# First loads of an attention kernel in order of need, and modulation columns turned on VectorE

## The chip, the cores and the metric

The kernel runs on one core of one Trainium2 chip. The metric is the device time of one execution in microseconds (us). Times of a trace are counted from its first instruction; the span of a trace (first to last instruction) is about 1.3 us shorter than the time of the same run. Each time below is a median of several executions. "Half clock" below means that the trace shows a granted TensorE clock of 0.50 of full speed.

## The reference, cut to what matters

```python
mod = (_silu(c) @ w_mod).reshape(c.shape[0], 6, 1, -1)      # c: 1 x 640, w_mod: 640 x 3840
sa, ca, ga, sb, cb, gb = (mod[:, i] for i in range(6))       # cut: written out in the reference
h = _layernorm(x) * (1 + ca) + sa                            # x: 1 x 2048 x 640
x = x + ga * _A_ref(h, A_k_cache, A_v_cache, A_wq, A_wo)     # 32 heads of 128, 2048 keys each
h = _layernorm(x) * (1 + cb) + sb
return x + gb * _B_ref(h, B_w1, B_w2, B_w3, B_w4)            # a smaller gated part, not touched here
```

`_A_ref` is attention: queries `h @ wq`, scores against the keys of the head, softmax, a weighted sum of the head's values, and the output weights `wo`. It is nearly all of the time. Of the six modulation rows, `sa` and `ca` are needed at once; the other four are needed only late.

## The kernel before

Instructions are not written in order. A helper records each one, `P.op(engine, function, estimated ns, reads, writes, priority, ...)`, and a scheduler of the kernel's own puts them in order and adds the waits. `from_slot(n)` means "not before the n-th exponential on ScalarE", counted from 0; there are `NP` = 8 exponentials for each step of one head and 512 queries. The parts that the change and the argument touch:

```python
def load_k(h, prio, gate=(), need=()):      # the keys come transposed, in four transfers on SP's queue
    b = h % NKV                             # NKV = 5 buffers for keys and values
    for i in range(4):
        dmaT(lambda e, i=i: e.dma_start_transpose(K_ap[b][:, i * 512:(i + 1) * 512].unsqueeze(1), A_k_cache[0, h, i * 512:(i + 1) * 512, :]),
             128, gate if i or h else (), (K[b][i],), prio + (1.6 if h == 0 and i else 0) + 0.01 * i, need)

def load_v(h, prio, eng="SP", gate=(), need=(), after=()):   # the values come as they lie, 512 KB in one transfer
    b = h % NKV
    dma(eng, lambda e: e.dma_start(V_ap[b][:, :, 0:128], A_v_cache[0, h].rearrange("(t p) d -> p t d", p=128)), 512, gate, (V[b],), prio, need, after)

# inside load_head(h): wm[2] is a part of the first modulation weights
if h in (1, 2, 3):
    load_k(h, (-294, -291, -289)[h - 1], (wm[2],), () if h < 3 else from_slot(12))
    load_v(h, (-292, -290, -289.5)[h - 1], gate=(wm[2],))

# the input of the late modulation, 640 values of bfloat16, goes to DRAM and comes back on all 128 partitions
def s_rows(slot):
    dma("SP", lambda e: e.dma_start(s_scr.ap().rearrange("(k p) -> p k", p=128), s_bf.ap, allow_slow_non_contiguous=True), 80, (s_bf,), (s_line,), slot * 1.0, from_slot(slot))
    dma("SP", lambda e: e.dma_start(s_row.ap, s_scr.ap().unsqueeze(0).to_broadcast([128, D])), 160, (s_line,), (s_row,), slot * 1.0)

# the matmul that needs the values: every one of a head waits for the head's whole buffer V[b]
P.op("PE", pv, 2 * MM(129), (pt, V[b]), (o[bk],), kb, accum=True)
# ... cut: scores, exponentials, output projection, normalisation, the second part and the tail
```

## Time and profile before

| what | value |
|---|---|
| time | 1377.84 us (1377.21 to 1378.32), three runs |
| the run that the profile shows | 1380.32 us, span 1379.0, mean granted TensorE clock 0.996 |
| TensorE busy | 99% of the span |
| stop 1, 18.33 to 21.80 us | values of head 0, then half clock to 27.4 |
| stop 2, 113.69 to 116.28 us | all engines quiet, then half clock to 119.5 |

The lines are in the prediction. They are read from the engine that is nearly always busy (TensorE) to its few stops, and from each stop to what ended it and to the clock behind it.

### The profile page before, as it was taken

The page shows a single profiled execution, that of the slowest core. Times are in us where ns is not written, and L with a number is a line of the kernel's source. Part 1 is how long each engine was busy: PE and PEld are TensorE (multiplying, and loading weights), DVE is VectorE, ACT ScalarE, POOL GpSimd, SP SyncE. Part 2 cuts the span into 40 slices and gives each one's busy share as a digit, 9 for nine tenths or more (in the row PEclk, how much of TensorE's full clock was granted, in tenths as well). Part 3 has the DMA queues.
Part 4 walks back from the last instruction along what each step waited for, and adds up shares of the span by engine and source line. Part 5 has one row for each costly group of instructions (what it writes and reads, how often), then busy time and mean ns, then how long its engine had stood idle before and what let it go on. Part 6 is the DMA issues. An engine that isn't in the chain of part 4 may idle for free.

```text
span 1379.0 us, 29901 instructions
## 1 busy us (share of the span) xinstructions
PE 1368.1 (99%) x13099; PEld 944.8 (69%) x13099; DVE 567.5 (41%) x1431; ACT 1101.6 (80%) x1144; POOL 107.1 (8%) x93
## 2 busy tenths in 40 slices
PE   8999999999999999999999999999999999999999
PEld 6766777677767777767776677767667766655665
DVE  4452444453333233233323332332333245799563
ACT  4987888888888888888888888888888888833322
POOL 0000000000000000000000000000333237500000
PEclk9999999999999999999999999999999999999999
DMA  9662624354213322151215121422227100441110
GB/s 203 121 119 44 121 42 81 83 106 81 47 35 62 82 46 37 24 97 35 39 32 108 36 47 36 85 59 47 55 56 125 43 13 16 113 88 41 42 44 31
DMA packets 273596, 90.39 MB, mean 66 GB/s; under 512 B 253425, under 2 KB 271538, under 8 KB 273458
## 3 DMA queue, kind: packets, MB, share of 16 engines
q1 hardware_dynamic: 270034, 85.75, 31.4%
q10 hardware_dynamic: 3280, 2.00, 0.7%
q8 instruction: 104, 1.70, 0.5%
q0 software_dynamic: 144, 0.66, 0.2%
q14 instruction: 34, 0.28, 0.1%
HBM read 41.68 MB, written 2.63 MB: 32 GB/s over the span
## 4 chain that ended last, share of the span: by engine, by line
PE 98%; DMA 1%; DVE 1%; ACT 0%; issue 0%; POOL 0%; POOLq 0%
PE f_O L799 34%; PE f_S L780 32%; PE f_M L704 10%; PE f_M L734 10%; PE f_S L976 2%; PE f_M L976 2%; PE f_O L963 2%; PE f_S L963 2%; PE f_S L914 1%; DMA f_KV<-in_A_v_cache_dram 1%; PE f_S L937 1%; PE f_M L937 1%; PE f_O L914 1%; DVE f_small L497 0%; PE f_S L438 0%; PE f_O L734 0%
## 5 line engine op out<-in xcount | busy, mean ns | idle before, releaser
L782 ACT ACTIVATE f_PQ<-f_S 128x1024 bf16<-128x1024 f32 x1024 | 1041.6, 1024 | 148.6 <-PE f_S L780 135.3
L799 PEld LDWEIGHTS f_O<-f_KV,f_PQ 128*128 128x128 bf16 x8192 | 591.9, 98 | 235.2 <-DMA f_KV<-in_A_v_cache_dram 4.0
L780 PE MATMUL f_S<-f_PQ,f_KV 128*128 128x512 bf16 x2048 | 728.6, 380 | 3.0 <-ACT f_PQ L782 3.0
L799 PE MATMUL f_O<-f_KV,f_PQ 128*128 128x129 bf16 x8192 | 715.1, 220 | 3.5 <-DMA f_KV<-in_A_v_cache_dram 3.5
L742 DVE TENSOR_TENSOR f_y<-f_M,f_y 128x320 f32<-128x320 f32 x192 | 94.4, 492 | 507.2 <-PE f_M L734 507.2
L734 PE MATMUL f_M<-f_wo,f_OO 128*128 128x320 bf16 x992 | 272.9, 299 | 0.0
L780 PEld LDWEIGHTS f_S<-f_PQ,f_KV 128*128 128x128 bf16 x2048 | 197.1, 98 | 32.4 <-ACT f_PQ L782 4.1
L704 PE MATMUL f_M<-f_hT,f_wq 128*128 128x512 bf16 (+1 forms) x640 | 175.8, 378 | 0.2 <-DVE f_tmp L745 0.2
L734 PEld LDWEIGHTS f_M<-f_wo,f_OO 128*128 128x128 bf16 x992 | 96.2, 98 | 28.5
L808 DVE TENSOR_TENSOR f_OO<-f_O,f_rl 128x256 bf16<-128x256 f32 x256 | 108.4, 423 | 8.2
L708 DVE CAST f_PQ<-f_M 128x512 bf16<-128x512 f32 x127 | 87.8, 691 | 53.6 <-PE f_M L704 53.1
L536 POOL TENSOR_TENSOR f_y<-f_y,f_mod 128x640 f32<-128x640 f32 x32 | 49.1, 1542 | 782.3 <-DVE f_y L742 782.3
L704 PEld LDWEIGHTS f_M<-f_hT,f_wq 128*128 128x128 bf16 x640 | 62.4, 98 | 63.8 <-DVE f_tmp L745 0.6
L806 DVE RECIPROCAL f_rl<-f_O 128x2 f32<-128x2 f32 x256 | 43.5, 170 | 39.1 <-PE f_O L799 34.9
L966 ACT ACTIVATE f_OO<-f_S 128x512 bf16<-128x512 f32 x28 | 16.7, 597 | 43.6 <-PE f_S L963 43.6
L740 DVE COPY f_y<-f_M 128x320 f32<-128x320 f32 x32 | 15.7, 492 | 55.3 <-PE f_M L734 52.0
L497 DVE BATCH_NORM_STATS2 f_small<-f_y 128x6 f32<-128x320 f32 (+1 forms) x72 | 32.5, 480 | 9.4 <-DMA f_y<-in_A_x_dram 7.6
L976 PE MATMUL f_M<-f_KV,f_OO 128*128 128x320 bf16 x224 | 31.7, 299 | 0.0
L976 PE MATMUL f_S<-f_KV,f_OO 128*128 128x320 bf16 x224 | 31.7, 299 | 0.0
L542 ACT ACTIVATE f_xn<-f_y,f_small 128x640 bf16<-128x640 f32 x10 | 9.1, 915 | 25.7 <-DVE f_small L521 25.7
L648 DVE TENSOR_REDUCE f_small<-f_tmp 128x1 f32<-128x640 f32 x20 | 16.4, 820 | 29.9 <-ACT f_PQ L782 29.9
L966 ACT ACTIVATE f_OO<-f_O 128x512 bf16<-128x512 f32 x28 | 16.7, 596 | 14.1 <-PE f_O L963 14.1
(140 smaller groups left out, 529.6 us busy)
## 6 DMA issues: line engine op xcount, KB each, us to landing
f_KV<-in_A_v_cache_dram SPq DMA_DIRECT2D x31, 512.0 KB, 4.7
f_wo<-in_A_wo_dram SPq DMA_DIRECT2D x8, 640.0 KB, 4.2
f_wq<-in_A_wq_dram SPq DMA_DIRECT2D x7, 640.0 KB, 4.5
f_xin<-in_A_x_dram SPq DMA_DIRECT2D x13, 320.0 KB, 3.8
out_dram<-f_xin SPq DMA_DIRECT2D x15, 160.0 KB, 1.8
f_KV<-in_B_w_dram SPq DMA_DIRECT2D x5, 432.0 KB, 3.9
f_KV<-in_A_k_cache_dram SPq DMA_TRANSPOSE x128, 2.7
f_OO<-f_OO SPq DMA_TRANSPOSE x128, 2.5
```

Of the source, the lines that this page charges most:

```text
L536: P.op(eng, lambda e: e.tensor_tensor(out=out, in0=a, in1=b, op=op), COST[eng][0], rd, wr, prio, lat=300 if eng == "POOL" else None, dual= ...
L704: P.op("PE", lambda e, i=i, kk=kk, mm=mm, a=a, z=z: e.matmul(mm[:, 0:z - a], wq_t[g % 2][:, kk, hh * 128:(hh + 1) * 128], hT_t[ch][:, kk, ...
L708: P.op("DVE", lambda e: e.tensor_copy(q.ap, m.ap), 690, (m,), (q,), s * NP - 90)
L734: P.op("PE", lambda e, m=m, qt=qt, hf=hf, hh=hh: e.matmul(m[:, 0:HD], OT_ap[gs][:, qt, hh, :], wo_t[g % 2][:, hh, hf * HD:(hf + 1) * HD], ...
L742: P.op("DVE", lambda e, m=m, yt=yt: e.tensor_tensor(out=yt.ap, in0=m[:, 0:HD], in1=yt.ap, op=ALU.add), 490, (m, yt), (yt,), s * NP - 60)
L780: P.op("PE", lambda e, sp=sp, r=r, kt=kt: e.matmul(sp[:, r * QC:(r + 1) * QC], K_ap[b][:, kt * 128:(kt + 1) * 128], q.ap, start=True, stop ...
L782: x = P.op("ACT", lambda e, sp=sp, pt=pt: e.activation(pt.ap.rearrange("p k q -> p (k q)"), sp.ap, ACT.Exp, scale=SCALE), 1021, (sp,), (pt ...
L799: ins = e.matmul(o[bk][:, w * 129:w * 129 + 129], pt[:, r, qt * 128:(qt + 1) * 128], V_ap[b][:, u, 0:129], start=(u == 0 and w == 0), stop ...
L806: P.op("DVE", lambda e, ov=ov, i0=i0: e.reciprocal(rl_t[:, i0:i0 + 2].unsqueeze(2), ov[:, 0:258].rearrange("p (u d) -> p u d", u=2)[:, :, ...
L808: evac.append(P.op("DVE", lambda e, ov=ov, i0=i0, bk=bk: e.tensor_tensor(out=On_ap[gs][:, 2 * bk:2 * bk + 2, hh, :], in0=ov[:, 0:258].rear ...
L963: P.op("PE", lambda e, m=m, f=f, kk=kk: e.matmul(m.ap, w3_ap[:, kk, f * 128:(f + 1) * 128], nT_ap[ch][:, kk, :], start=(kk == 0), stop=(kk ...
L976: P.op("PE", lambda e, f=f, hf=hf: e.matmul(m[:, hf * 512:hf * 512 + HD], gT_ap[:, f, i * 128:(i + 1) * 128], w4_ap[f][:, hf * HD:(hf + 1) ...
```

## The change

The intent is to take away both stops.

- **First loads in order of need.** The values of head 0 come in two halves, and the early matmuls wait for the first half alone. The keys of heads 1 and 2 and their values wait for the first exponential. Query weights of heads 2 and 3, and the second chunk of the input, are held back too, and the first keys of head 0 now wait for a part of the modulation weights, as its other keys did. The values of head 3, which stood in SP's queue ahead of that chunk's transposes, now stand behind them and behind the keys of head 3.
- **Modulation.** The input is no longer sent through DRAM two bytes at a time. It is computed again, on all partitions, from a broadcast of `c`: an exponential on ScalarE, then three VectorE operations on 128x640. The finished columns are turned by one VectorE transpose and written in four pieces. The broadcast is released at exponential 64, where the two-byte write had been released at 70.

```diff
-    load_v(0, -296.5, "ACT", after=(ln0[1],))
+    for a, z, t in ((0, NKT // 2, v0a), (NKT // 2, NKT, V[0])):
+        dma("ACT", lambda e, a=a, z=z: e.dma_start(V_ap[0][:, a:z, 0:128], A_v_cache[0, 0, a * 128:z * 128].rearrange("(t p) d -> p t d", p=128)),
+            256, (), (t,), -296.5, after=(ln0[1],))
...
-            load_k(h, (-294, -291, -289)[h - 1], (wm[2],), () if h < 3 else from_slot(12))
-            load_v(h, (-292, -290, -289.5)[h - 1], gate=(wm[2],))
+            load_k(h, (-294, -291, -289)[h - 1], need=from_slot((0, 0, 12)[h - 1]))
+            load_v(h, (-292, -290, -288)[h - 1], need=from_slot((0, 0, 12)[h - 1]))
...
-    load_wq(0, 1, HG, -296.8, eng="ACT", after=(ln0[0],))
+    load_wq(0, 1, 2, -296.8, eng="ACT", after=(ln0[0],))
+    load_wq(0, 2, HG, -291, eng="POOL", need=from_slot(1))
...
-                640, (wm[3], wm[4]), xs + held, -294)
+                640, (), xs + held, -292, need=(lambda: ln0[2],))
...
-                    P.op("PE", pv, 2 * MM(129), (pt, V[b]), (o[bk],), kb, accum=True)
+                    P.op("PE", pv, 2 * MM(129), (pt, v0a if s == 0 and u < NKT // 2 else V[b]), (o[bk],), kb, accum=True)
...
     def s_rows(slot):
-        (the two-byte write and its read back, shown above)
+        c_bf = T(flat(nTx_t)[:, D:2 * D])
+        dma("SP", lambda e: e.dma_start(c_bf.ap, c[0:1, :].to_broadcast([128, D])), 160, (), (c_bf,), slot * 1.0, from_slot(slot))
+        P.op("ACT", lambda e: e.activation(tmp[0].ap, c_bf.ap, ACT.Exp, scale=-1.0), act(D), (c_bf,), (tmp[0],), slot + 9.0, need=from_slot(slot + 9))
+        P.op("DVE", lambda e: e.tensor_scalar_add(out=tmp[1].ap, in0=tmp[0].ap, scalar1=1.0), 600, (tmp[0],), (tmp[1],), slot + 12.0, need=from_slot(slot + 12))
+        P.op("DVE", lambda e: e.reciprocal(tmp[0].ap, tmp[1].ap), 825, (tmp[1],), (tmp[0],), slot + 14.0, need=from_slot(slot + 14))
+        P.op("DVE", lambda e: e.tensor_tensor(out=s_row.ap, in0=tmp[0].ap, in1=c_bf.ap, op=ALU.mult), 825, (tmp[0], c_bf), (s_row,), slot + 20.0, dual=True, need=from_slot(slot + 20))
... cut: the columns of all four rows in one tile `cols`, its transpose and the four writes; small bookkeeping
```

More of the change, by code (lines that the diff above doesn't have):

```diff
@@ L406, in fast_path @@
                                            fill=1.0, base=0, channel_multiplier=1), 300, (ident,), (ident,), -298)
+    v0a = T()
     def v_ones(i):
-        P.op("POOL", lambda e: e.memset(V_ap[i][:, :, 128:130], 1.0), 200, (), (V[i],), -297 + i)
+        P.op("POOL", lambda e: e.memset(V_ap[i][:, :, 128:130], 1.0), 200, (), (V[i],) + ((v0a,) if i == 0 else ()), -297 + i)
     for i in range(NKV):
@@ L587, in ln1 @@
                 if k % 2:
-                    P.op("ACT", lambda e, k=k: e.activation(hT_t[0][:, k, :], hslice(k, 0, 4), ACT.Identity,
+                    h = P.op("ACT", lambda e, k=k: e.activation(hT_t[0][:, k, :], hslice(k, 0, 4), ACT.Identity,
                                                             scale=caT[:, k:k + 1], bias=saT[:, k:k + 1]),
                          770, (hp[k], saT, caT), (hT[0][k],), -280 + k)
+                    ln0.append(h)
                 else:
@@ L607, in load_k @@
             dmaT(lambda e, i=i: e.dma_start_transpose(K_ap[b][:, i * 512:(i + 1) * 512].unsqueeze(1), A_k_cache[0, h, i * 512:(i + 1) * 512, :]),
-                 128, gate if i or h else (), (K[b][i],), prio + (1.6 if h == 0 and i else 0) + 0.01 * i, need)
+                 128, gate, (K[b][i],), prio + (1.6 if h == 0 and i else 0) + 0.01 * i, need)
     def load_v(h, prio, eng="SP", gate=(), need=(), after=()):
@@ L627, in fast_path @@
     ln1(0, -280)
-    s_scr = nc.dram_tensor("s_scratch", [D], BF16)
     m_scr = nc.dram_tensor("m_scratch", [4, D], F32)
-    s_line, s_row = T(), T(flat(nTx_t)[:, 0:D])
+    s_row = T(flat(nTx_t)[:, 0:D])
     nT_old[3] = lambda: (s_row,)
     wT = [[T() for _ in range(KT)] for _ in range(2)]
+    MODS = (2, 4, 3, 5)
+    cols, turned = T(small(32)), T(small(32))
+    P.op("DVE", lambda e: e.memset(cols.ap, 0.0), 100, (), (cols,), 60.0, need=from_slot(60))
     def s_rows(slot):
-        dma("SP", lambda e: e.dma_start(s_scr.ap().rearrange("(k p) -> p k", p=128), s_bf.ap, allow_slow_non_contiguous=True), 80, (s_bf,), (s_line,), slot * 1.0, from_slot(slot))
-        dma("SP", lambda e: e.dma_start(s_row.ap, s_scr.ap().unsqueeze(0).to_broadcast([128, D])), 160, (s_line,), (s_row,), slot * 1.0)
+        c_bf = T(flat(nTx_t)[:, D:2 * D])
[3 more added lines that the diff above has]
+        P.op("DVE", lambda e: e.reciprocal(tmp[0].ap, tmp[1].ap), 825, (tmp[1],), (tmp[0],), slot + 14.0, need=from_slot(slot + 14))
+        P.op("DVE", lambda e: e.tensor_tensor(out=s_row.ap, in0=tmp[0].ap, in1=c_bf.ap, op=ALU.mult), 825, (tmp[0], c_bf), (s_row,), slot + 20.0, dual=True,
+             need=from_slot(slot + 20))
     def modulation(n, p, slot):
         i = n % 2
-        col, line = T(small(KT)), T()
         for j in range(KT):
+            r = n * KT + j
             dmaT(lambda e, j=j: e.dma_start_transpose(w_half[i][:, j, :].unsqueeze(1), w_mod[:, p * D + j * 128:p * D + (j + 1) * 128]),
@@ L647, in modulation, with mod_rows @@
                  (wT[i][j], s_row), (tmp[j % 2],), slot + 20.0, dual=True, slack=1500.0, need=from_slot(slot + 20 + NP * j))
-            P.op("DVE", lambda e, j=j: e.tensor_reduce(out=col[:, j:j + 1], in_=tmp[j % 2].ap, op=ALU.add, axis=mybir.AxisListType.X), 825,
-                 (tmp[j % 2],), (col,), slot + 20.0, need=from_slot(slot + 22 + NP * j))
+            P.op("DVE", lambda e, j=j, r=r: e.tensor_reduce(out=cols[:, r:r + 1], in_=tmp[j % 2].ap, op=ALU.add, axis=mybir.AxisListType.X), 825,
+                 (tmp[j % 2],), (cols,), slot + 20.0, need=from_slot(slot + 22 + NP * j))
         if p == 4:
-            P.op("DVE", lambda e: e.tensor_scalar_add(out=col.ap, in0=col.ap, scalar1=1.0), 170, (col,), (col,), slot + 20.0)
-        dma("SP", lambda e: e.dma_start(m_scr.ap()[n].rearrange("(j q) -> q j", q=128), col.ap, allow_slow_non_contiguous=True), 80, (col,), (line,), slot + 24.0)
-        dma("SP", lambda e: e.dma_start(mod_t[p][:], m_scr.ap()[n:n + 1, :].to_broadcast([128, D])), 320, (line,), tuple(mod[p]), slot + 24.0)
-    load_v(0, -296.5, "ACT", after=(ln0[1],))
+            P.op("DVE", lambda e: e.tensor_scalar_add(out=cols[:, n * KT:n * KT + KT], in0=cols[:, n * KT:n * KT + KT], scalar1=1.0), 170, (cols,), (cols,), slot + 20.0)
+    def mod_rows(slot):
+        P.op("DVE", lambda e: e.transpose(turned.ap, cols.ap), 200, (cols,), (turned,), slot * 1.0, need=from_slot(slot))
+        lines = tuple(T() for _ in range(4))
+        to = m_scr.ap().rearrange("n (j b i) -> b (n j) i", b=4, i=32)
+        for b in range(4):
+            dma("SP", lambda e, b=b: e.dma_start(to[b], turned[b * 32:b * 32 + 4 * KT, :]), 10, (turned,), (lines[b],), slot * 1.0)
+        for n, p in enumerate(MODS):
+            dma("SP", lambda e, n=n, p=p: e.dma_start(mod_t[p][:], m_scr.ap()[n:n + 1, :].to_broadcast([128, D])), 320, lines, tuple(mod[p]), slot + 1.0)
+    for a, z, t in ((0, NKT // 2, v0a), (NKT // 2, NKT, V[0])):
+        dma("ACT", lambda e, a=a, z=z: e.dma_start(V_ap[0][:, a:z, 0:128], A_v_cache[0, 0, a * 128:z * 128].rearrange("(t p) d -> p t d", p=128)),
+            256, (), (t,), -296.5, after=(ln0[1],))
     def load_head(h):
@@ L677, in fast_path @@
     load_group(1)
-    s_rows(70)
-    for n, p in enumerate((2, 4, 3, 5)):
+    s_rows(64)
+    for n, p in enumerate(MODS):
         modulation(n, p, 80 + 40 * n)
+    mod_rows(80 + 160 + 30)
     TAIL = ("A0 B0 B1 A1 B2 B3 B4 A2 WO I3 B5 B6 C0 B7 D0 D1 D2 D3 B8 C1 B9 B10 A3 D4 B11 "
```

## The prediction

> **What bounds the kernel now.** I read the page first, then TensorE's waits from 14 us on, then a table of stretches, then the timeline around the two bad stretches.
>
> The page says that TensorE is the bound, and that little else is left to take:
>
> ```profile
> PE 1368.1 (99%) x13099; PEld 944.8 (69%) x13099; DVE 567.5 (41%) x1431; ACT 1101.6 (80%) x1144; POOL 107.1 (8%) x93
> ...
> PE 98%; DMA 1%; DVE 1%; ACT 0%; issue 0%; POOL 0%; POOLq 0%
> ```
>
> The second line is the chain that ended last: 98% of it is matmul. So only two things can shorten the time: time in which TensorE stands still, and time in which its matmuls run slower than they can. The waits of TensorE after 14 us (columns: who waited for whom, us in total, how often, longest) show how few stops there are:
>
> ```profile
> PE f_O L799 <- DMA f_KV<-in_A_v_cache_dram: 3.5, 1, 3.5
> PE f_S L780 <- ACT f_PQ L782: 3.0, 3, 2.6
> PE f_M L937 <- ACT f_PQ L924: 0.3, 1, 0.3
> PE f_M L704 <- DVE f_tmp L745: 0.2, 1, 0.2
> ```
>
> Two stops matter, one of 3.5 us and one of 2.6 us. The table of stretches (us from the start, length, busy time and count for five engines, granted TensorE clock, DMA share, GB/s) shows that each costs more than its length, since the clock is at half afterwards:
>
> ```profile
> 18.30:21.80 3.50, 0.03 (x1) 0.00 (x1) 0.00 (x0) 1.02 (x1) 0.00 (x0) 0.82 1.12 196
> 21.80:27.40 5.60, 5.60 (x35) 3.94 (x36) 5.29 (x22) 2.05 (x2) 0.00 (x0) 0.50 1.43 181
> 27.40:35.50 8.10, 8.10 (x86) 5.67 (x85) 4.06 (x17) 7.44 (x8) 0.00 (x0) 1.00 0.93 178
> ...
> 113.70:116.30 2.60, 0.02 (x1) 0.02 (x2) 0.49 (x1) 1.09 (x2) 0.00 (x0) 0.96 0.00 0
> 116.30:119.50 3.20, 3.20 (x20) 2.26 (x21) 0.00 (x0) 1.87 (x2) 0.00 (x0) 0.50 0.56 81
> 119.50:1200.00 1080.50, 1080.28 (x10851) 759.99 (x10848) 390.64 (x926) 952.10 (x953) 102.36 (x76) 1.00 0.31 60
> ```
>
> TensorE does nothing in the first and fourth row, and runs at clock 0.50 in the second and fifth. The last row is the other 80% of the kernel: no idle time worth naming, full clock.
>
> **Stop 1: the values of head 0.** The list of transfers up to 70 us has, for the load of these values:
>
> ```profile
> f_KV<-in_A_v_cache_dram ACTq DMA_DIRECT2D x1, 512.0 KB, 12.8
> ```
>
> It is issued at 8.92 us and lands at 21.75; the first matmul on values starts at 21.80. Later loads of the same 512 KB take a median of 4.7 us. The trace's packets tell why: from 2 to 28 us the DMA engines are at 90% or more, because the keys of heads 0, 1, 2, the rows of the second chunk (640 KB) and three heads of query weights (480 KB) run beside it. Loss: 3.47 us idle, and 5.56 us at half clock, half of it lost (2.78). Together 6.25 us.
>
> **Stop 2, at 113.7 us.** In the timeline:
>
> ```profile
> 115.06 0.34 SPq L638 DMA_DIRECT2D f_nTx<-s_scratch  x1
> 115.20 1.94 ACT L782 ACTIVATE f_PQ<-f_S 128x1024 bf16<-128x1024 f32 x2 [3.63 <-PE f_M L734]
> 115.39 0.49 DVE L740 COPY f_y<-f_M 128x320 f32<-128x320 f32 x1 [3.28 <-remote]
> ...
> 116.28 0.61 PE L780 MATMUL f_S<-f_PQ,f_KV 128*128 128x512 bf16 x1 [2.59 <-ACT f_PQ L782]
> ```
>
> ACT's scores were complete at about 113.3, VectorE's input at 113.7, yet three queues move only at 115.1 to 115.4. What ends at just that moment is the write of the modulation input to DRAM, issued at 97.95 as 640 elements of two bytes: the trace has its data packets done by 101 us, and the signal of its completion at 115.04. I take it that this pending write held the other engines' signals back. It is an inference from one coincidence. Loss: 2.59 us idle plus half of 3.2 us at half clock (1.6), together 4.2 us. The profile is not its cause: the profiled run took 1380.32 us and plain ones 1377.84, and without 4.2 us it would have beaten the plain ones.
>
> **What the Trainium skill says.** (1) "TensorE: Matmul & The Clock Gate", Part 1: the clock falls to half after an idle window of about 3.4 us and returns after a busy one. The trace agrees: half-clock stretches of 6.83 and 3.41 us, though a stop of 2.59 us was enough for one. (2) "DMA: Bandwidth & Descriptors", Queues, rings and completion order: each DMA engine takes turns between queues, packet by packet. So traffic on SP's and GpSimd's queues stretches a load on ACT's; 12.8 us against 4.7 agrees. (3) "Perfetto Trace Analysis", DMA Instruction — HWDGE: the signal waits until the write is confirmed, "a surprisingly long delay especially when the write target is HBM". The 14 us from last packet to signal agree; that other engines are held back is on no page. (4) "VectorE: DVE Perf Modes", The three transpose paths: VectorE's transpose works on 32x32 blocks, which is why the new code writes four pieces; no run before has it.
>
> **The change part by part.** The order of TensorE's instructions is unchanged, instruction by instruction, so the work of the bound is the same.
>
> (a) First loads. The values come as two halves of 256 KB, and matmuls on key tiles 0 to 7 wait for the first alone. Beside them there is now 160 KB of query weights in place of 480, no second chunk before 12.7 us (it waits for a ScalarE step that ended at 12.7) and no keys of heads 1 and 2 before the first exponential, whose end is at about 16.1. Estimate: from 8.2 us on some 1.2 MB (512 KB values, 512 KB keys of head 0, 160 KB weights) are to be moved before all are in; at the 190 GB/s that this phase ran at before, that ends at about 14.5 us, and the first half nearer 13. They are needed at 18.2 and about 21. Stop 1 goes: -6.25 us. The keys of head 0 now all wait for the third part of the modulation weights (8.15 us); the first is needed at 14.49, and the like transfer before took 5.4 us from issue, so about 13.6: just in time.
>
> (b) Modulation. Removed: the two-byte write and its read back, four writes of 4-byte columns. Added: one broadcast load, one exponential of 128x640 on ScalarE (by its 0.92 us row of that size, in a stage where eight exponentials take 8.2 of 9.26 us), about three wide VectorE operations of 0.8 us (VectorE is 41% busy), one 32x32 transpose, four small writes and four broadcasts. None is needed before the seventh group of heads, beyond 800 us. Nothing of it is on the path; what counts is that stop 2 goes: -4.2 us.
>
> (c) What is delayed. Values of head 1 follow its keys on SP: four transposes at 1.3 us from 16.15, so issued at about 21.4 and, at 4.7 us, landed at 26.1. They are needed at 32.65 - 6.25 = 26.4. Values of head 3 now stand behind four transposes of the second chunk and the keys of head 3: issued at some 38.5, landed at 43, needed at 49.0 - 6.25 = 42.75. Two near ties: I put +0.8 us for both.
>
> Sum: 1377.84 - 6.25 - 4.2 + 0.8 = 1368.2 us.
>
> **The rivals.** First: **a new wait takes the old one's place** at head 1's or head 3's values or head 0's keys. For: the near ties in (c), and any stop of some 2.5 us also brings the half clock. Against: the queues are much emptier. It would give back 1 to 5 us: 1369 to 1373. Second: **stop 2 has another cause** than the two-byte write and stays, or the new writes bring it back. For: the later 4-byte writes took 5 to 9 us to land and stopped nothing. Against: the coincidence within 0.2 us. Result about 1372.4. Third: **ScalarE or VectorE becomes the bound** in the stage with the added operations. The 1 us of slack per eight exponentials speaks against it; at worst some tenths. Fourth: **the transfers were hidden anyway**: ruled out for the values, as TensorE waited for them.
>
> **Range and chances.** About 65% that both stops go (1366.8 to 1370), 25% that one stays or a new wait of several us appears (1370 to 1374), the rest odd cases on either side. With this upward skew I say 1368.4, and 1366.6 to 1372.8 for eight in ten. TensorE's own work at full clock leaves a floor of about 1367.4 (1377.84 - 10.45), so a gain of 2% (27.6 us) is out of reach, and a loss of 2% would need five stops like the first: within 2% at 0.98.
>
> **What would show it.** Right: no TensorE wait on values before 25 us, the first half of the values landed before 18 us, clock 1.00 from 14.5 us to the tail, no stop near 110 us, and the first matmul of head 1 on values at about 26.4. Wrong: a TensorE wait on a key or value load between 14 and 45 us with a half-clock stretch behind it; or a stop of all engines near the first modulation columns although no two-byte write is left; or a span that shrinks by only one of the two losses.

## The result, and the profile after

| kernel | time, us | profiled run |
|---|---|---|
| before, same rounds | 1378.0 (1377.21 to 1378.32, four runs) | span 1379.0, clock 0.996 |
| changed | 1375.42 (1375.12 to 1375.85, four runs) | 1375.85 us, span 1374.5, clock 0.999 |

The ratio is 0.9982, with an interval of 0.9965 to 1.0: within 2%. A ratio here and below is the mean time of one kernel's fast runs over the mean of the other's of the same rounds (in the experiments, without the first run of each), so it is not quite the ratio of the medians. The gain is 2.6 us where 9.4 had been predicted, and the interval just reaches 1.0, no gain.

The page of the changed kernel, its first busy line and its chain:

```profile
PE 1352.1 (98%) x12865; PEld 941.7 (69%) x13099; DVE 572.6 (42%) x1436; ACT 1102.4 (80%) x1145; POOL 108.0 (8%) x94
...
PE 95%; DMA 2%; issue 1%; DVE 1%; SPq 1%; ACT 0%
```

The count of 12865 matmuls is not less work: some matmul records are missing, while the weight loads are 13099 in both traces. So the busy time of PE can't be compared, but the weight loads can be used to lay the two traces side by side. In the chain a DMA and SP's queue now have a share.

TensorE's waits from 14 us on, in the changed kernel (columns as before):

```profile
PE f_O L821 <- DMA f_KV<-in_A_v_cache_dram: 3.8, 2, 3.6
PE f_M L756 <- DVE f_y L762: 0.6, 1, 0.6
PE f_O L821 <- DVE f_OO L830: 0.4, 1, 0.4
```

The first line looks like stop 1 of before, since it names the same tile, but it is another head. The table of stretches (from, to and length; busy time of PE, PEld, DVE, ACT, POOL; clock, DMA share, GB/s):

```profile
14.00:42.37 28.37, 27.72 (x271) 18.50 (x274) 14.63 (x53) 25.91 (x27) 0.86 (x1) 1.00 0.94 163
42.37:46.00 3.63, 0.01 (x2) 0.01 (x1) 0.30 (x1) 1.02 (x1) 0.00 (x0) 0.94 0.98 220
46.00:49.00 3.00, 3.00 (x20) 2.17 (x21) 0.80 (x2) 1.02 (x1) 0.00 (x0) 0.50 0.96 335
```

Up to 42.37 us TensorE now works with hardly a gap: the halves of head 0's values landed at 13.22 and 15.01, and stop 1 is gone. Then it stands still for 3.62 us, with the DMA engines 98% busy, and runs at half clock behind that. SP's queue tells which load this was. Here it is in the changed kernel, then before (start, length, what was issued):

```profile
27.93 0.58 SPq L615 DMA_DIRECT2D f_KV<-in_A_v_cache_dram  x1
28.56 6.80 SPq L600 DMA_TRANSPOSE f_hT<-f_xn  x4
35.41 5.18 SPq L610 DMA_TRANSPOSE f_KV<-in_A_k_cache_dram  x4
40.63 1.46 SPq L615 DMA_DIRECT2D f_KV<-in_A_v_cache_dram  x1
```

```profile
30.02 2.10 SPq L612 DMA_DIRECT2D f_KV<-in_A_v_cache_dram  x2
32.17 8.43 SPq L597 DMA_TRANSPOSE f_hT<-f_xn  x4
40.64 5.17 SPq L607 DMA_TRANSPOSE f_KV<-in_A_k_cache_dram  x4
```

Before, the values of heads 2 and 3 went out together at 30 us. After, those of head 3 wait for eight transposes and are issued at 40.63; they land at 45.95, and TensorE goes on at 46.00. The whole set of keys and values of heads 0 to 3 had landed at 47.06 before and has at 45.95 after: TensorE asks for it some 6 us sooner and gets it only 1.1 us sooner.

The second and third wait have one cause. VectorE's timeline, then TensorE's (start, length, instruction, and in brackets the idle time before it with what ended it):

```profile
105.87 4.15 DVE L646 RECIPROCAL f_tmp<-f_tmp 128x640 f32<-128x640 f32 x1 [1.78 <-ACT f_PQ L804]
109.94 0.43 DVE L762 COPY f_y<-f_M 128x320 f32<-128x320 f32 x1
```

```profile
110.42 0.45 PE L756 MATMUL f_M<-f_wo,f_OO 128*128 128x320 bf16 x2 [0.62 <-DVE f_y L762]
...
111.62 0.73 PE L821 MATMUL f_O<-f_KV,f_PQ 128*128 128x129 bf16 x6 [0.38 <-DVE f_OO L830]
```

The reciprocal of the new modulation holds VectorE for 4.15 us. The copy out of the accumulator and the normalisation of a head queue up behind it, and TensorE waits for both. Nothing else stops near 110 us.

Laid side by side by the starts of the same weight loads, the two traces give this account (negative: the changed kernel is ahead). The last column is the running sum, and it ends at the difference of the two spans, 4.5 us:

| from | what | us | sum |
|---|---|---|---|
| start to 42 us | no stop 1 (-6.32), an earlier start (-0.84), a wait for the values of head 1 (+0.37) | -6.79 | -6.79 |
| 42 to 49 us | wait for the values of head 3, and half clock | +5.21 | -1.58 |
| 109 to 112 us | behind the reciprocal | +1.43 | -0.15 |
| from 113 us | no stop 2 | -4.33 | -4.48 |

### The profile page after: what moved, and what is told of

Its sections match the earlier page's. It is cut to its first block, busy times and chain, and to the rows that moved or that the text cites. A ratio compares the mean times of both kernels' runs of the same rounds, so it can differ in the third digit from the quotient of the medians.

```text
span 1374.5 us, 29675 instructions
## 1 busy us (share of the span) xinstructions
PE 1352.1 (98%) x12865; PEld 941.7 (69%) x13099; DVE 572.6 (42%) x1436; ACT 1102.4 (80%) x1145; POOL 108.0 (8%) x94
## 4 chain that ended last, share of the span: by engine, by line
PE 95%; DMA 2%; issue 1%; DVE 1%; SPq 1%; ACT 0%
PE f_O L821 35%; PE f_S L802 29%; PE f_M L756 10%; PE f_M L726 9%; PE f_S L998 2%; PE f_M L998 2%; PE f_O L985 2%; PE f_S L985 2%; PE f_S L936 1%; PE f_S L959 1%; PE f_M L959 1%; DMA f_KV<-in_A_v_cache_dram 1%; PE f_O L936 1%; SPq L610 1%; DMA f_W<-in_w_mod_dram 0%
## 5 line engine op out<-in xcount | busy, mean ns | idle before, releaser
L802 PE MATMUL f_S<-f_PQ,f_KV 128*128 128x512 bf16 x1857 | 664.9, 379 | 4.1 <-DMA f_KV<-in_A_k_cache_dram 0.4
L726 PE MATMUL f_M<-f_hT,f_wq 128*128 128x512 bf16 (+1 forms) x609 | 169.7, 378 | 1.8 <-DVE f_tmp L767 0.2
```

What stands on the lines that cost most here:

```text
L726: P.op("PE", lambda e, i=i, kk=kk, mm=mm, a=a, z=z: e.matmul(mm[:, 0:z - a], wq_t[g % 2][:, kk, hh * 128:(hh + 1) * 128], hT_t[ch][:, kk, ...
L802: P.op("PE", lambda e, sp=sp, r=r, kt=kt: e.matmul(sp[:, r * QC:(r + 1) * QC], K_ap[b][:, kt * 128:(kt + 1) * 128], q.ap, start=True, stop ...
```

## The experiments

Theory: three things ate the gain. The values of head 3 come too late in SP's queue (5.2 us); the one-piece reciprocal delays VectorE (1.4 us); and the profiled run of before was a slow one, so the gain to be had was smaller than the trace showed. The rivals: the stop at 42 us is not one of order but of DMA bandwidth, and moves elsewhere whatever the order; and stop 2 had another cause than the two-byte write, so that another part of the change removed it. Eleven runs were made in three calls, each call on another chip, all with correct results. The kernel before ran in each call: 1377.91, 1380.99 and 1379.39 us. It differs by 3 us between calls, so ratios are compared rather than times.

**1. The kernel before, once more.** No edit.

> The kernel before, unchanged, to see whether its second stop is always there. If the two-byte write of the modulation input causes it, its trace shows again a stop of all engines near 114 us that ends when that write's completion is signalled, and granted clock about 0.996 to 0.998. If that stop was an accident of the one traced run, TensorE has no gap over 1 us between 27 and 1180 us and the span is some 2 to 4 us shorter than the 1379.0 us of the first trace. Ratio to the kernel before 1.000 either way.

Measured 1377.07 us (1374.57 to 1378.74), ratio 1.0 (0.9985 to 1.0015), clock of the trace 1.000. The waits in this trace, which has a span of 1374.0 us instead of 1379.0:

```profile
PE f_S L780 <- DMA f_KV<-in_A_k_cache_dram: 2.7, 2, 1.8
PE f_S L780 <- ACT f_PQ L782: 1.7, 2, 1.4
```

There is no wait for values: those of head 0 landed at 17.97, not 21.75. Stop 2 is there but only 1.44 us long, and neither stop was followed by half clock. So both losses that the prediction measured are real but vary from run to run, and the one trace it had was one of the bad ones.

**2. The values of head 3 on GpSimd's queue.** One line of the changed kernel:

```diff
-            load_v(h, (-292, -290, -288)[h - 1], need=from_slot((0, 0, 12)[h - 1]))
+            load_v(h, (-292, -290, -288)[h - 1], "POOL" if h == 3 else "SP", need=from_slot((0, 0, 12)[h - 1]))
```

> The changed kernel, with the load of head 3's values issued from GpSimd's queue after the 13th exponential instead of from SP's behind the transposes of the second chunk and of head 3's keys. Theory (these values are late because of their place in SP's queue): issued at about 26 us, landed before 34, needed at 42.4; the 3.6 us stop and the half-clock stretch after it go; 3.6 to 5.1 us less than the changed kernel, so about 1370.5 to 1372 us. Rival (the engines of the DMA are simply behind, and something else is late in its stead): a new wait of 1 us or more on keys or on the second chunk between 30 and 46 us, and a time within 1.5 us of the changed kernel's 1375.4.

Measured 1372.57 us (1371.97 to 1373.95), ratio 0.9968 (0.9955 to 0.9981). The longest waits left:

```profile
PE f_O L821 <- DMA f_KV<-in_A_v_cache_dram: 1.0, 1, 1.0
PE f_M L756 <- DVE f_y L762: 0.6, 1, 0.6
```

The values of head 3 were issued at 28.58 and landed at 35.7, long before their need. The 1.0 us is another wait: the values of head 2, which now share the DMA engines with them, landed at 35.35 for a need at 34.5. Most of the stop is a matter of order in one queue, and a smaller part of it moves elsewhere, as the rival had it.

**3. The values of head 3 early on SP's own queue.**

```diff
-            load_v(h, (-292, -290, -288)[h - 1], need=from_slot((0, 0, 12)[h - 1]))
+            load_v(h, (-292, -290, -289.5)[h - 1], need=from_slot(0))
```

> The changed kernel, with head 3's values back in the place that they had before: on SP's queue right behind head 2's values, ahead of the transposes of the second chunk. Theory: values of head 3 land by 35 us, so the stop at 42.4 us goes, but the four transposes of the second chunk and the keys of head 3 come 0.6 us of issue and some 1.5 us of transfer later than in the changed kernel, where head 3's first keys were ready only about half a us before use: a wait of 0.5 to 2 us on those keys near 38.6 us is likely. About 1371.5 to 1373.5 us. Rival (SP order is of no matter, the stop comes from elsewhere): the stop at 42 us stays and the time is 1375.4.

Measured 1373.2 us (1372.59 to 1374.26), ratio 0.9973 (0.9959 to 0.9986). The stop on the values is gone; in its place TensorE stood 1.80 us at 39.21, on the keys of head 3, which now queue behind. The stop is thus movable by order alone. The shorter stop also cost less than its share: no stop of 1.95 us or less in any trace was followed by half clock.

**4. The reciprocal in four pieces of 160 columns, four exponentials apart.**

```diff
-        P.op("DVE", lambda e: e.reciprocal(tmp[0].ap, tmp[1].ap), 825, (tmp[1],), (tmp[0],), slot + 14.0, need=from_slot(slot + 14))
+        quarters = tuple(T(tmp[0].ap[:, i * 160:(i + 1) * 160]) for i in range(4))
+        ... one reciprocal for each quarter i, at slot + 14 + 4 * i; the multiply after them moves from slot + 20 to slot + 30
```

> The changed kernel, with the one reciprocal over 640 columns (4.15 us on VectorE in its trace) cut into four over 160 columns, each released by another exponential. Theory (one long instruction holds up the evacuations of TensorE's results behind it, which cost 0.62 and 0.38 us of gaps near 110 us and about 1.4 us in all): quarters of about 1.05 us, no gap over 0.2 us near 110 us, 1.0 to 1.5 us less: about 1374.2 us. Rival (the gaps come from the write and read traffic of that stage, or the added work itself): the gaps stay, 1375.4 us.

Measured 1375.39 us (1374.69 to 1376.76), ratio 0.9987 (0.9974 to 1.0). The four pieces took 1.14 to 1.16 us each, and both gaps behind VectorE near 110 us were gone. But the time shows no gain over the 1375.42 of the changed kernel, which ran earlier. In this trace the stop on head 3 was 4.06 us, with another 0.99 us at 26.67, for the values of head 1. So the cause is shown by the gaps that went; what it is worth in time this run does not show, as the interval of its ratio (some 1.8 us to either side) is wider than the 1.4 us in question.

**5. The first loads alone** (the kernel before with the five pieces of the diff above that concern loads, and their bookkeeping, but no new modulation).

> The kernel before, with the new first loads alone (values of head 0 in two parts, keys of heads 1 and 2 after the first exponential, the second chunk and two heads of query weights later, head 3's values behind its keys); the modulation as before. Theory: the first stop goes (as in the changed kernel), the stop at head 3's values of about 3.6 us comes, and the stop of 1.4 to 2.6 us at the end of the two-byte write near 110 us stays; no 4 us reciprocal. Against the changed kernel: plus that last stop, minus 1.4 us of the reciprocal, so about 1375.5 to 1377.5 us. Rival (the stop near 110 us has nothing to do with the two-byte write): no such stop, 1374 us.

Measured 1380.43 us (1378.95 to 1382.34), ratio 1.0004 (0.9984 to 1.0024).

```profile
PE f_S L786 <- ACT f_PQ L788: 4.1, 4, 3.3
PE f_O L805 <- DMA f_KV<-in_A_v_cache_dram: 3.9, 1, 3.9
```

The first line is stop 2 (114.24 to 117.50, when the two-byte write completed at 116.20), the second the values of head 3; 1.14 us more went to the values of head 1. Stop 1 was removed, and within the noise its gain was given back by these waits. One thing here is unlike the other traces: stop 2, though 3.27 us long, was not followed by half clock (the granted clock is 1.00 from 114.2 to 124 us).

**6. The new modulation alone** (the changed kernel with those five pieces taken back).

> The kernel before, with the new modulation alone, first loads as before. Theory: the first stop varies as it does in the kernel before (0.5 to 3.5 us, with or without the half clock), no stop when a two-byte write ends since there is none, but gaps of about 1 us behind the long reciprocal: 0.5 to 3 us less than the kernel before of the same rounds, spread of runs as wide as there. Rival (the two-byte write is innocent): the 1.4 us of the reciprocal comes on top, 1 to 1.5 us slower than the kernel before.

Measured 1377.38 us (1374.17 to 1379.83), ratio 0.9979 (0.9958 to 1.0001). The trace has stop 1 (5.82 us, the longest seen) and the 0.61 and 0.37 us behind the reciprocal, and nothing that looks like stop 2. With the first loads of before, stop 2 still goes: it belongs to the modulation part. To judge by the ratios, the net gain of the whole change (0.9982) is this part's, though each of these intervals reaches 1.0.

**7. The two-byte write earlier.** The kernel before with one number changed, which sends the write some 28 us sooner:

```diff
-    s_rows(70)
+    s_rows(40)
```

> The kernel before, with the two-byte write of the modulation input and its read back released at the 41st exponential in place of the 71st, some 31 us earlier. Theory: the stop of all engines follows the write: its completion comes 14 to 17 us after its issue, near 80 us, all engines stand still for 1 us or more just before it, and nothing stops near 110 us. Rival (the stop at 110 to 114 us belongs to what happens there, instruction fetch or the traced run): it stays there and none appears near 80 us. Time as the kernel before either way.

Measured 1378.16 us (1377.16 to 1381.56), ratio 0.9992 (0.9972 to 1.0012). From the timeline of all engines:

```profile
89.05 3.77 ACT L782 ACTIVATE f_PQ<-f_S 128x1024 bf16<-128x1024 f32 x4 [2.67 <-PE f_M L734]
89.39 0.34 SPq L638 DMA_DIRECT2D f_nTx<-s_scratch  x1
89.70 0.49 DVE L740 COPY f_y<-f_M 128x320 f32<-128x320 f32 x1 [5.54 <-PE f_M L734]
90.13 0.61 PE L780 MATMUL f_S<-f_PQ,f_KV 128*128 128x512 bf16 x2 [1.95 <-ACT f_PQ L782]
```

The write was issued at 70.45 and its data packets were done at 76.31. It is complete when its semaphore has counted to 16. The trace holds ten of these signals, from 87.16 to 89.38, and SP's read back, which waits for them all, went out at 89.39. The expectation had put this near 80 us. ScalarE, SP's queue, VectorE and TensorE all stood and started again together between 89.05 and 90.13, and nothing stopped near 114. The stop went where the write went. In the three traces with the write at its old place, the read back went out at 115.06 and ScalarE moved again at 115.20 (before); at 111.28 and 111.82 (before again); at 116.22 and 116.42 (first loads alone). So in all four traces ScalarE moved again between 0.3 us before and 0.5 us after the read back, much as the prediction had seen it in one. The tie between write and stop is shown.

By what path is not shown. ScalarE and VectorE waited in these stops for TensorE's semaphore, not for a DMA. The first increments of it that the traces hold in these stops came at 115.18, 111.79, 116.31 and 89.03 us, 0.6 to 2.4 us after the last matmul before the stop had started. One rival is untested: in each of the four traces a 16 KB packet of an instruction queue began while the write was pending (at 111.82, 109.44, 112.55 and 83.75 us). Such packets come every 10 to 15 us anyway, and one at 111.8 us in the trace of the new modulation alone was followed by no such stop. The earlier write also had a cost of its own: SP's queue stood behind it until 89.39, and TensorE then waited 1.13 us, until 103.12, for a transpose of that queue.

**8. Head 3's values on GpSimd's queue, but later (after exponential 17 instead of 12), with the reciprocal in quarters.**

> The changed kernel with both cures: head 3's values from GpSimd's queue, now after the 18th exponential so that they do not run beside head 2's (which came 0.94 us late in the run with them after the 13th), and the reciprocal in quarters. Theory: no gap over 0.6 us from 17 us to 1170 us; 1.4 and some 0.9 us less than the 1372.6 us of that run: about 1370.3 us, within 1369.5 to 1371.3. Rival (there is always something late in the crowded first 50 us): a new wait of 1 us or more, 1372 us or above.

Measured 1373.62 us (1373.06 to 1374.42), ratio 0.9955 (0.9936 to 0.9974). It missed its aim. The load was issued at 33.5 and now ran beside the second chunk's last transpose and the first keys of head 3, which landed at 40.87 and 41.1: a new stop of 2.45 us at 38.78, with half clock from 1.3 us after its end. Holding a load until just before its need is no cure when others need the same engines then.

**9. The changed kernel again.**

> The changed kernel, unchanged, on the chip of the two runs beside it, since the kernel before read 1377.9 us on one chip and 1381.0 on another. Theory: the stop at head 3's values (3.6 us or more, with or without a half-clock stretch) and the two gaps of 0.6 and 0.4 us behind the long reciprocal are there in every profile; some 1375.4 us, 2 to 5 us less than the kernel before beside it.

Measured 1377.38 us (1375.77 to 1379.05), ratio 0.998 (0.9962 to 0.9998), the ratio of the result (0.9982) once more. The stop on head 3 was 3.86 us with 6.8 us of half clock; the 0.61 and 0.37 us behind the reciprocal were there again.

**10. The values of head 3 in two halves, between the four transposes of its keys.** As the changed kernel already does it for head 0, matmuls on key tiles 0 to 7 wait for the first half alone:

```diff
-            load_v(h, (-292, -290, -288)[h - 1], need=from_slot((0, 0, 12)[h - 1]))
+            if h == 3:
+                for a, z, t, pr in ((0, NKT // 2, v3a, -288.985), (NKT // 2, NKT, V[3], -288.975)):
+                    dma("SP", lambda e, a=a, z=z: e.dma_start(V_ap[3][:, a:z, 0:128], A_v_cache[0, 3, a * 128:z * 128].rearrange("(t p) d -> p t d", p=128)),
+                        256, (), (t,), pr, need=from_slot(12))
+            else:
+                load_v(h, (-292, -290)[h - 1], need=from_slot(0))
```

> The changed kernel, with head 3's values loaded in two halves as head 0's are: the first behind the second of the four transposes of head 3's keys, the second behind the third; same queue, same bytes. Theory (order of need within SP's queue decides, not the amount of traffic): the first half is issued near 38.0 us and landed by 42.3, when it is needed; the third and fourth part of the keys come about 1 us later than before but have 2 us to spare. The stop at 42.4 us shrinks from 3.6 us to under 0.8 us, no half clock: 3 to 5 us less than the changed kernel beside it. Rival (the transfers as a whole cannot keep up in the first 45 us): a stop of 2 us or more on these values or on keys stays, less than 1.5 us gained.

Measured 1372.77 us (1372.14 to 1373.73), ratio 0.995 (0.9932 to 0.9968), 4.6 us below the changed kernel. No wait on values of head 3 and no half clock; 0.84 us are left at 43.38, on keys. This is about the size of the stop, measured as time: 4.6 us against the 5.2 of the traces.

**11. The same, with the values of head 1 one place earlier in SP's queue and the reciprocal in quarters.**

```diff
-                load_v(h, (-292, -290)[h - 1], need=from_slot(0))
+                load_v(h, (-293.975, -290)[h - 1], need=from_slot(0))
```

> As the run before it, and head 1's values ahead of the fourth transpose of head 1's keys (they came 0.2 to 1.1 us late in the traces of the changed kernel and its kin, the keys had 5 us to spare), and the reciprocal in quarters. Theory: each cure keeps its own worth: 1.0 to 1.4 us for the quarters and 0.2 to 1.0 us for head 1's values, so 1.2 to 2.4 us less than the run before it; no gap over 0.9 us after 17 us; about 1369 to 1370 us where the changed kernel reads 1375.4. Rival (a wait removed here comes back behind): less than 0.5 us gained on the run before it.

Measured 1371.81 us (1370.68 to 1372.73), ratio 0.9941 (0.9922 to 0.9959). The longest waits left after 12 us:

```profile
PE f_S L810 <- DMA f_KV<-in_A_k_cache_dram: 0.8, 1, 0.8
PE f_S L810 <- issue: 0.8, 2, 0.6
PE f_S L810 <- ACT f_PQ L812: 0.4, 2, 0.2
```

There is no wait for VectorE near 110 us and none for values. It gains 0.96 us on experiment 10, less than expected (1.2 to 2.4). This is the best version found, and it beats both kernels: 7.6 us below the kernel before and 5.6 below the changed one, in the same call.

## Why the prediction was wrong

It said 1368.4 us, with 1366.6 to 1372.8 as its range; 1375.42 came, outside. It said within 2%, and that was so. By its own steps:

1. **What bounds the kernel, and its two stops:** right. TensorE's order was unchanged, and both stops went in the changed trace.
2. **Stop 1, -6.25:** right in mechanism and in size for that trace (-6.32 by the aligned traces). The first half landed at 13.22 for "nearer 13", the second at 15.01 for "about 14.5", the first keys at 13.53 for "about 13.6".
3. **Stop 2, -4.2, laid to the two-byte write:** right. It moved with the write (experiment 7), stayed when the write stayed (5) and went when only the new modulation came in (6); -4.33 in the aligned traces. One reading was off: the later 4-byte writes took 8.1 to 11.7 us to land in that trace, not "5 to 9". That they stopped nothing, though under way for so long, is one more reason to call the path open.
4. **"Two near ties: I put +0.8 us for both": the step that failed first.** Head 1's values were right in this trace (landed 25.73 for a predicted 26.1, a gap of 0.2 us); in three others with the same loads (experiments 4, 5 and 9) TensorE waited 0.9 to 1.1 us for them. Head 3's were wrong. The issue came at 40.63 instead of "some 38.5" and the landing at 45.95 instead of 43, while the need came at 42.37 instead of 42.75. A tie of a quarter of a microsecond became a stop of 3.62 us, and with the half clock behind it 5.2 us. The step that failed is the price of SP's queue ahead of this load. The "some 38.5" is about what four transposes of head 2's keys, four of the second chunk and four of head 3's keys take at 1.3 us each, counted on from 21.4 us. But the first transpose behind each of the two 512 KB loads held the queue for 2.57 and 2.85 us instead of 1.26, so that 2.9 us came on top. The trace of before had shown such delays: four transposes of the second chunk took 8.43 us there. What holds the queue at these places stays open. The prediction's own first rival had named the wait, and its list of what would make it wrong had too; the mistake was to give it a quarter of the chances at a cost that it had priced too low in the sum. Its "any stop of some 2.5 us also brings the half clock" held for eight of the nine stops of 2.45 us or more in all traces, but not for the one of 3.27 us (experiment 5).
5. **"About three wide VectorE operations of 0.8 us ... Nothing of it is on the path": wrong.** The reciprocal took 4.15 us, five times the size assumed. It was not on the path by what reads it, but by the queue of its engine: two short VectorE steps that TensorE does need stood behind it. It cost 1.43 us in the aligned traces; the same two gaps are in all six traces with the one-piece reciprocal, and in none of the three with quarters. How much time the quarters win by themselves stays open: the one run that has them alone (experiment 4) can't resolve it.
6. **"Sum: 1377.84 - 6.25 - 4.2 + 0.8": wrong in its base.** Both losses were read off a run of 1380.32 us and taken from a median of 1377.84. The prediction saw that the profiled run was slower, and used it only to clear the profiler of stop 2. With the loss and the base from the same run, the terms close: 1380.32 - 6.79 + 5.21 + 1.43 - 4.33 = 1375.84, and the profiled run of the changed kernel took 1375.85. Experiment 1 confirms the reason: another trace of the same kernel had a stop 2 of half that length and no wait on values.

So the miss of 7.0 us is made of these: 4.4 for head 3's values (5.2 less the 0.8 allowed), 1.4 for the reciprocal and 2.5 for the base, together 8.3. Against them stand 0.7 by which the first 42 us and stop 2 came out better than told (most of it the earlier start), 0.2 by which the stated time lay above the sum, and 0.4 by which the median of the changed kernel lay below its profiled run.

What stays open: what holds SP's queue behind the 512 KB loads, why stop 1 varies (of the four traces with the old first loads, two had waits of 3.5 and 5.8 us for head 0's values and two had none, but 2.2 and 2.7 us of waits for keys), and by what path the pending write stops other engines.

## What to carry to other kernels

When a change brings the bound engine forward, every later load is needed sooner by as much; list the issue and need time of each load in the queue, and count a load with less slack than the queue's own scatter as late, at the price of the wait and of the slower clock that may follow it. An operation that nobody on the path reads can still delay the path if it is long and shares an in-order engine with short operations that the path needs; cut it up, and look up its real duration by operation, not by size. Take losses and base from the same run, and look at two traces before calling a stop a fixed cost.

## What the Trainium skill lacked or had wrong

- "TensorE: Matmul & The Clock Gate", Part 1, has the clock fall after an idle window of about 3.4 us and calls the window free-running. The traces agree in the lengths of the slow stretches (always 3.41 or 6.83 us), but stops of 2.45 and 2.59 us were followed by one, stops up to 1.95 us never were, and one of 3.27 us was not. It would help to say that a gap shorter than the window can cost a half-clock stretch, but need not.
- "VectorE: DVE Perf Modes", First, the fixed hardware budget, says that the reciprocal is an iterative divide with a repeat count of 8, but gives no duration. Here it took 4.15 us for 128x640 in float32, 1.15 us for 128x160 and 0.17 us for 128x2, while a multiply or reduction of 128x640 took about 0.8 us.
- "Perfetto Trace Analysis", DMA Instruction — HWDGE, warns of a long delay of the completion signal of a write to HBM. The runs agree: 640 elements of two bytes had their packets done 12.7 to 15.5 us before the last of the signals that the trace holds. What the pages say of late signals concerns the signals of DMAs. That near the end of such a delay waits for TensorE's semaphore are released late as well is on no page: stops of 1.4 to 3.3 us in four traces, moving with the write. The later writes of four-byte elements took 8 to 12 us from issue to landing and stopped at most 0.5 us.
- "DMA: Bandwidth & Descriptors", Queues, rings and completion order, has the engines take turns between queues, packet by packet. The runs agree, and give the price: with the values of head 3 moved to GpSimd's queue, those of head 2 on SP's queue landed 0.8 us after their need, 7.0 us after their issue in place of 5.2.
